# Causal decayed attention in front of a Strassen FFN: sequence chunks of 128 positions become chunks of 64 that lie two by two in the halves of the partitions

## The chip, the cores and the metric

The kernel runs on one core of one Trainium2 chip. The metric is the device time of one execution in microseconds (us). TensorE (PE) multiplies; it keeps a weight tile in its 128x128 array and streams columns past it, and its results go to PSUM, which has eight banks. VectorE (DVE) and ScalarE (ACT) take results out of PSUM, GpSimd (POOL) works on SBUF alone, and DMA queues are fed by SyncE (SP), ACT and POOL. Here a PE "record" is one line of the profile, a weight load with the matmul that uses it; each fp32 matmul of the program leaves two records, and a transpose through PE leaves one.

## The reference

```python
scores = scale * np.matmul(q, k.transpose(0, 1, 3, 2))       # q, k, v: 8 x 8 x 576 x 64 (batch, head, position, dim)
Dmat = np.where(rel >= 0, gamma[:, None, None] ** rel[None, :, :], 0.0)
attn = np.matmul(scores * Dmat[None], v)                     # gamma = 1 - 2 ** (-5 - head)
x = attn.transpose(0, 2, 1, 3).reshape(4608, 512)
out = (((x @ w1) * (x @ w2)) @ w3) @ w_out                   # 512 -> 1024 -> 1024 -> 512
```

All in float32. The decay is split by position into a factor on q and one on v, so inside a chunk only the causal mask is left, and everything before the chunk is summed in a 64x64 state (k transposed times v) for each head.

## The kernel before, in words

**Attention.** The 8 batches are 4 pairs. A pair's 576 positions are cut into a short chunk of 64 (c = 0) and four full ones of 128 (c = 1 to 4); `g` counts the 20 steps of (pair, chunk). A step has 16 units: 2 batches `b`, 4 pairs of heads `p`, 2 heads `j`. Head j of a pair lies in half j of the partitions (`heads[j]`). For a full chunk one step has four matmul stages of 16 matmuls, so 32 records each:

- `score` (L224): for every unit keys times queries, 64 rows deep, 128x128 out. The two heads use the two row halves of the array at once. The results (`sc`) are multiplied by the causal mask on DVE into `pm` (L236), four instructions of 128x512.
- `state` (L240): keys times values, 128 rows deep, 64x64 out, the two heads in the two column halves, summed in PSUM over a pair's chunks in `st` (one bank); ACT copies the sum to `sb` (L259) for the next chunk. The last chunk of a pair has none.
- `pv_state` (L264): state times queries, 64 deep, 64x128 out, four units at once in the four quarters of the array, into two banks `xps`.
- `pv` (L278): masked scores times values, 128 deep, 64x128 out, two column halves, added to `xps`; `evict` copies `xps` to `xT` on ACT (L306).

In the short chunk `score` and `pv` and `state` are 64x64 and use two quarters at once. Keys and queries are transposed for `score` either by PE (`front`, L207) or by DVE on blocks of 32 (`front_blocks`, L185).

**FFN.** Tokens go through Strassen products: `up` (L507) and, from the second half on, `up2` (L1008, weights streamed from HBM through the ring `ra`) for w1 and w2, `down` (L625) for the product w3*w_out, which is computed once (`w3_mm`). Each product is a run of records on the full array, 192 columns in `up` and `up2`, 256 in `down`; DVE, ACT and POOL add the products up.

**Order.** It is written out by hand, and each engine runs its instructions in the order of the program. The first pair's attention stands between weight conversions on DVE and ACT. From the second pair on, a step deals out some FFN items with `work(n)`, then runs `pv(g)` with its eviction, then `state(g + 1)` and `score(g + 1)` in one block, and goes on with the next items. The next chunk's loads, scalings and transposes stand between the items (`aside`, `beside`, `loads`). PSUM: `st` one bank, `acc` seven buffers; in the second half five, with two of `seed`.

Of the kernel before, what the change touches and what calls it, by code (L numbers as in the profile page):

```python
# [19 lines left out]
def kernel(  # L20
# [31 lines left out]
    G = NB2 * NC  # L52
    NB = 3
# [27 lines left out]
    acc = acc_part.enter_context(tc.tile_pool(name="acc", bufs=7, space=PSUM))  # L81
# [5 lines left out]
    def load(g, names, engine=nc.sync):  # L87
        i, c = divmod(g, NC)
        sz = sizes[c]
        src = {"k": k, "q": q, "v": v}  # L90
        for nm in names:
            t = pools["ld"].tile([P, 2 * H, D], F32, tag="ld_" + nm, name="ld_" + nm)
            engine.dma_start(
                t[:sz], src[nm][2 * i:2 * i + 2, :, starts[c]:starts[c] + sz, :].rearrange("b h p d -> p (b h) d"))
            live[nm, g] = t
# [11 lines left out]
                            base=0, pattern=[[1, P]], channel_multiplier=-1)  # L107

# [98 lines left out]
    def front(g, names="kq"):  # L207
        c = g % NC
        sz = sizes[c]
# [14 lines left out]
    def score(g):  # L224
        c = g % NC
        sz = sizes[c]
        kT, qT = live["kT", g], live["qT", g]
        pm = pools["fr"].tile([P, 2, 2, NP, P], F32, tag="pm", name="pm", bufs=1)
        for b in range(2):
            sc = [acc.tile([P, NP, P], F32, tag="acc", name="sc") for j in range(2)]  # L230
            for p in range(NP):
                for j, hs in enumerate(heads):
                    nc.tensor.matmul(sc[j][:sz, p, :sz], kT[hs, b, p, :sz], qT[hs, b, p, :sz],  # L233
                                     start=True, stop=True)
            for j in range(2):
                nc.vector.tensor_mul(pm[:sz, b, j, :, :sz], sc[j][:sz, :, :sz],  # L236
                                     mask[:sz, :sz].unsqueeze(1).to_broadcast([sz, NP, sz]))
        live["pm", g] = pm

    def state(g):  # L240
        c = g % NC
        sz = sizes[c]
        if c == NC - 1:
            return
        vs = live["v", g]
        kn = live["k", g]
        if c == 0:
            live["st"] = st_ps.tile([P, 2, NP, D], F32, tag="st", name="st")
        st = live["st"]

        for b in range(2):
            for p in range(NP):
                for j, hs in enumerate(heads):
                    h = b * H + 2 * p + j
                    nc.tensor.matmul(st[hs, b, p, :], kn[:sz, h, :], vs[:sz, h, :],  # L255
                                     start=(c == 0 and b == 0 and p == 0), stop=(c == NC - 2),
                                     skip_group_check=True)
        sb = pools["fr"].tile([P, 2, NP, D], F32, tag="sb", name="sb")
        nc.scalar.copy(sb, st)  # L259
        live["sb", g + 1] = sb  # L260

    bank_order = [(b, n) for b in range(2) for n in range(2)]

    def pv_state(g):  # L264

        sz = sizes[g % NC]
        qT = live["qT", g]

        banks = live["xps", g] = [acc.tile([P, 2, 2, P], F32, tag="acc", name="xps") for r in range(2)]
        if g % NC:  # L270
            for m, (b, n) in enumerate(bank_order):
                for r, j in ((0, 0), (0, 1), (1, 0), (1, 1)):
                    p = 2 * r + n
                    nc.tensor.matmul(banks[r][heads[j ^ r], b, n, :sz], live["sb", g][heads[j], b, p, :],  # L274
                                     qT[heads[j], b, p, :sz], start=(m == 0), stop=False,
                                     skip_group_check=True)

    def pv(g):  # L278

        if ("xps", g) not in live:  # L280
            pv_state(g)
# [3 lines left out]
        vs, pm, banks = live["v", g], live["pm", g], live["xps", g]  # L285
# [9 lines left out]
        for m, (b, n) in enumerate(bank_order):  # L295
            for r in range(2):
                for half in range(2):
                    p, j = 2 * r + n, half ^ r
                    nc.tensor.matmul(banks[r][heads[half], b, n, :sz], vs[:sz, b * H + 2 * p + j, :],  # L299
                                     pm[:sz, b, j, p, :sz], start=(c == 0 and m == 0), stop=True,  # L300
                                     skip_group_check=True)

        def evict():
            for x, to, fr, n in parts:
                for r in range(2):
                    nc.scalar.copy(  # L306
                        x[:, 2 * r:2 * r + 2, :, to:to + n].rearrange("p n b s -> p b n s"),
                        banks[r][:, :, :, fr:fr + n])

        return evict  # L310

# [192 lines left out]
    def up(i, n, fp, conv=0, tail=True, first=False):  # L507
# [28 lines left out]
        c = ffn.tile([P, 4, 2, TB], F32, tag="c", name="c", bufs=1)  # L536
        p1 = product(None, "A11", "B11")
        nc.scalar.copy(c[:, 0], p1)

# [7 lines left out]
        plus(p7 if first else product(None, "S3", "T3"), 2, 1)  # L547
        p5 = product(None, "S1", "T1")
# [4 lines left out]
        nc.scalar.copy(c[:, 0], p1)  # L553
        product(p5, "S4", "B22")
        plus(p5, 1, 1)

# [68 lines left out]
    def down(x, y, then=None, last=False):  # L625
# [35 lines left out]
        C11, C12, C21, C22 = (0, 0), (0, 1), (1, 0), (1, 1)  # L661
        product(1, "A11", "B11")
# [5 lines left out]
        if second:  # L668
            store()
            finish()  # L670
        product(7, "S3", "T3")
        if second:
            multiply()
# [8 lines left out]
        nc.scalar.copy(ot[:, 0, 0], ps[2])  # L682
        early = second or last or g >= 2 * NC - 1
# [9 lines left out]
        if second:  # L693
            store()
        product(3, "S4", "B22", on=5)
# [46 lines left out]
    pv_state(1)  # L742
# [47 lines left out]
    owed.append(2)  # L790
    pv(4)()
# [129 lines left out]
    def open_second():  # L921
# [3 lines left out]
        acc = ctx.enter_context(tc.tile_pool(name="acc", bufs=5, space=PSUM, reuse_waits="tile"))  # L925
# [82 lines left out]
    def up2(gr, n):  # L1008
# [34 lines left out]

        p1 = acc.tile([P, 2, TB], F32, tag="acc", name="up")
# [6 lines left out]
        nc.scalar.copy(c[:, 3], p5)  # L1051
        finish()
# [12 lines left out]
        plus(p1, 0, add)  # L1065
        product(p5, "S4", "B22")
# [12 lines left out]
        if aside:  # L1079
            aside.pop(0)()  # L1080

# [37 lines left out]
    g = NC  # L1119
# [4 lines left out]
    state(NC)  # L1124
    score(NC)
    scale_blocks(NC + 1)
    in_blocks = [u >= 2 * NC - 3 for u in range(G)] + [False] * 2
    first_pair = range(NC, 2 * NC - 1)
    for g in first_pair:
        n = (1, 1, 2, 2)[g - NC]  # L1130
        if not in_blocks[g + 2]:
            load(g + 2, "k")
            load_blocks(g + 2, "q")
        scale(g + 1, "v")
        if not in_blocks[g + 1]:
            front(g + 1, "k")
            front_blocks(g + 1, "q")
        half = (n + 1) // 2
        if in_blocks[g + 1]:
            scale_blocks(g + 1)  # L1140
            work(n - 1)
            aside.extend(lambda nm=nm: front_blocks(g + 1, nm) for nm in "kq")
            work(1)
            while aside:
                aside.pop(0)()
            half = 0
        if in_blocks[g + 2] and g + 2 < 2 * NC:
            load_blocks(g + 2, "q")
            load_blocks(g + 2, "k")
        work(half)  # L1150
        pv(g)()
        load(g + 2, "v", nc.scalar if in_blocks[g + 2] else nc.sync)
        if in_blocks[g + 2] and (g + 2) % NC != NC - 1:
            load(g + 2, "k")
        state(g + 1)
        score(g + 1)
        if not in_blocks[g + 2]:
            scale_blocks(g + 2)
# [7 lines left out]
        if not in_blocks[g + 1]:  # L1166
            work(n // 2)

    g = 2 * NC - 1
    work(1)  # L1170
    load_blocks(g + 1, "q")
    pv(g)()
    load(g + 2, "v", nc.scalar)
    load(g + 2, "k")
# [5 lines left out]
    g = 2 * NC  # L1180
    work(1)
    rest()
    aside.append(lambda: front_blocks(g, "q"))
    work(1)
    while aside:
        aside.pop(0)()
    front(g, "k")
    ready = {2 * NC + 3: 1, 3 * NC + 1: 2, G - 1: 3}

    whole = range(2 * NC + 1, 2 * NC + 4)  # L1190
    load_blocks(g + 1, "q")
    state(g)
    score(g)
    add_group(0)
    dealt = [3, 4, 4, 3, 3, 7, 7, 3, 7, 7]
    for g in range(2 * NC, G):
        n = dealt[g - 2 * NC]
        if g + 1 < G:
            beside.extend(lambda j=j: scale(g + 1, "v", range(j, j + H // 2)) for j in (0, H // 2))
# [3 lines left out]
            if g - 1 in ready:  # L1203
                token_forms(ready[g - 1])
            for nm in "qk":
                blocks_in = nm == "q" or g + 1 not in whole
                if blocks_in:
                    aside.append(lambda nm=nm: front_blocks(g + 1, nm))
                work(1)
                while aside:  # L1210
                    aside.pop(0)()
                if not blocks_in:
                    while loads:
                        loads.pop(0)()
                    front(g + 1, "k")
                if g + 2 < G and not (nm == "k" and g + 2 in whole):
                    load_blocks(g + 2, nm)
            work(tail)
            for left in (loads, beside):
                while left:  # L1220
                    left.pop(0)()
        else:
            work(n)
        pv(g)()
        if g in ready:
# [58 lines left out]
```

## Time and profile before

| what | us |
|---|---|
| median of 3 runs (851.12, 847.23, 860.4) | 851.12 |
| the profiled execution: its own time | 850.68 |
| its span, first to last instruction | 848.9 |
| records of `score`, `pv`, `pv_state`, `state`: PE busy | 40.2, 36.8, 17.7, 19.0 |
| PE busy in `down`, `up2`, `up` (their groups added up; groups overlap a little) | 230, 313, 165 |

The page gives each engine's busy time and its share of the span; the chain of waits follows what ended last, back from the end; a group line gives the shape of the weights (rows*columns), the output, the number of records, the time in which at least one of them ran, the mean duration of one, and the engine's idle time before them. Records overlap, so a group's busy time is less than number times mean. In the timeline the first column is the start in us from the span's start, the second the time to the end of the last record merged into that line. In the table of windows each engine has its busy time and, in brackets, how many of its instructions lie there.

### The profile page before, as it was taken

How to read it: one execution, taken by the hardware profiler on the slowest of the kernel's cores; microseconds unless marked ns; L12 is line 12 of the kernel's file. 1: busy time of each engine (PE TensorE's matmuls, PEld its weight loads, DVE VectorE, ACT ScalarE, POOL GpSimd, SP SyncE). 2: the span in 40 equal slices, each digit the busy share in tenths (PEclk: the TensorE clock that was granted, in tenths of full speed). 3: DMA queues.
4: the chain of work that ended last, by engine and by line, in shares of the span. 5: the costliest groups of instructions: out<-in, count | busy, mean ns of one | idle time of the engine just before them, and what ended most of it. 6: DMA issues, size and time to landing. Idle time of an engine off the chain costs nothing.

```text
span 848.9 us, 15774 instructions
## 1 busy us (share of the span) xinstructions
PE 819.3 (97%) x6085; PEld 738.1 (87%) x6085; DVE 541.2 (64%) x887; ACT 283.2 (33%) x581; POOL 325.6 (38%) x330
## 2 busy tenths in 40 slices
PE   7899999999999999979998999999999999999998
PEld 6889999644989998869998889998899998899987
DVE  4899999991644477615657644759735768446653
ACT  4777556670111101033343024342034331033300
POOL 1100010001104181395545935556916468445500
PEclk8999999999999999999999999999999999999999
DMA  9995454436046487979786147787275452245401
GB/s 193 217 224 128 77 150 125 126 98 112 1 98 125 75 220 251 307 209 220 190 229 167 44 93 228 201 238 177 58 156 183 140 208 69 77 148 189 159 25 51
DMA packets 201291, 126.96 MB, mean 150 GB/s; under 512 B 161272, under 2 KB 183032, under 8 KB 201216
## 3 DMA queue, kind: packets, MB, share of 16 engines
q1 hardware_dynamic: 170944, 50.14, 29.1%
q0 software_dynamic: 11776, 63.71, 23.0%
q10 hardware_dynamic: 18496, 12.10, 5.3%
q8 instruction: 48, 0.79, 0.4%
q14 instruction: 27, 0.22, 0.1%
HBM read 103.62 MB, written 22.28 MB: 148 GB/s over the span
## 4 chain that ended last, share of the span: by engine, by line
PE 79%; DMA 7%; DVE 7%; issue 3%; SPq 2%; ACT 1%; POOL 0%; ACTq 0%; DVEq 0%; POOLq 0%
PE po L637 24%; PE up L1028 15%; PE up L524 13%; PE seed L1028 11%; PE ps L477 6%; DMA ld_v<-in_v_dram 3%; PE xps L299 3%; PE sc L233 3%; DMA ra<-kept 2%; PE xps L274 1%; SPq L171 1%; DVE c L529 1%; DVE ab L1003 1%; DMA bl_q<-in_q_dram 1%; PE st L255 1%
## 5 line engine op out<-in xcount | busy, mean ns | idle before, releaser
L637 PE MATMUL po<-w3o,ab 128*128 128x256 f32 x552 | 125.0, 381 | 1.4 <-DVE ot L641 0.5
L637 PEld LDWEIGHTS po<-w3o,ab 128*128 128x128 f32 x552 | 103.9, 190 | 17.4 <-DVE ot L641 1.2
L1033 POOL TENSOR_TENSOR cc<-cc 128x384 f32<-128x384 f32 x112 | 109.3, 1001 | 4.1 <-ACT cc L1051 2.4
L1040 DVE TENSOR_TENSOR cc<-seed,cc 128x384 f32<-128x384 f32 x88 | 48.7, 553 | 72.9 <-PE seed L1028 68.5
L181 POOL TENSOR_TENSOR bl_q<-bl_q,gqs 128x512 f32<-128x512 f32 (+1 forms) x30 | 30.8, 1048 | 127.7 <-DMA bl_q<-in_q_dram 91.8
L939 POOL DMA_DIRECT2D ra<-kept x54 | 30.6, 567 | 124.1 <-PE seed L1028 103.3
L1028 PE MATMUL up<-xT,ra 128*128 128x192 f32 x384 | 74.2, 330 | 0.6 <-DMA ra<-kept 0.6
L1040 DVE TENSOR_TENSOR cc<-up,cc 128x384 f32<-128x384 f32 x88 | 48.4, 550 | 36.8 <-PE up L1028 31.5
L524 PE MATMUL up<-xT,wA 128*128 128x192 f32 x384 | 70.4, 327 | 0.0
L529 DVE TENSOR_TENSOR c<-up,c 128x384 f32<-128x384 f32 x80 | 44.0, 550 | 38.9 <-PE up L524 38.3
L1028 PEld LDWEIGHTS up<-xT,ra 128*128 128x128 f32 x384 | 64.4, 192 | 2.0 <-DMA ra<-kept 0.9
L236 DVE TENSOR_TENSOR pm<-sc,mask 128x512 f32<-128x512 f32 (+1 forms) x80 | 45.4, 626 | 32.1 <-PE sc L233 32.0
L637 PE MATMUL po<-wB,forms 128*128 128x256 f32 x288 | 65.2, 379 | 0.5 <-DVE forms L611 0.5
L524 PEld LDWEIGHTS up<-xT,wA 128*128 128x128 f32 x384 | 63.4, 190 | 1.1 <-issue 0.5
L637 PEld LDWEIGHTS po<-wB,forms 128*128 128x128 f32 x288 | 54.6, 190 | 8.2 <-PE po L637 0.8
L1047 ACT COPY seed<-up 128x384 f32<-128x384 f32 x56 | 25.9, 463 | 100.1 <-PE up L1028 46.6
L1028 PE MATMUL seed<-e,ra 128*128 128x192 f32 x256 | 52.9, 337 | 5.2 <-DVE cc L1040 2.9
L1028 PE MATMUL up<-ra 128*128 128x192 f32 x288 | 55.1, 328 | 1.9 <-DMA ra<-kept 1.9
L477 PE MATMUL ps<-wo,w3T 128*128 128x512 f32 x128 | 55.1, 592 | 0.0
L204 POOL TENSOR_TENSOR ld_v<-ld_v,gk 128x1024 f32<-128x1024 f32 (+1 forms) x9 | 17.1, 1899 | 90.5 <-DMA ld_v<-in_v_dram 90.5
L679 DVE TENSOR_TENSOR ab<-ab,forms 128x512 f32<-128x512 f32 x17 | 17.1, 1008 | 53.3 <-PE po L637 53.3
L1028 PEld LDWEIGHTS seed<-e,ra 128*128 128x128 f32 x256 | 43.7, 194 | 7.8 <-DVE cc L1040 3.6
(127 smaller groups left out, 1597.2 us busy)
## 6 DMA issues: line engine op xcount, KB each, us to landing
ra<-kept POOLq DMA_DIRECT2D x54, 896.0 KB, 5.0
raw<-in_moe_w_dram SPq DMA_DIRECT2D x72, 128.0 KB, 3.0
bl_q<-in_q_dram SPq DMA_DIRECT2D x216, 32.0 KB, 3.2
out_dram<-ot ACTq DMA_DIRECT2D x54, 128.0 KB, 2.3
bl_k<-in_k_dram SPq DMA_DIRECT2D x136, 32.0 KB, 2.4
raw<-in_moe_w_dram SPq DMA_DIRECT2D x16, 256.0 KB, 6.0
ld_k<-in_k_dram SPq DMA_DIRECT2D x8, 512.0 KB, 5.9
raw<-in_moe_w_out_dram SPq DMA_DIRECT2D x32, 128.0 KB, 2.7
```

The lines of the kernel that those rows point to most:

```text
L181: nc.gpsimd.tensor_tensor(out=part, in0=part, in1=gqs[:, :, n0:n0 + n].unsqueeze(3).to_broadcast([P, NP, n, BL]), op=ALU.mult)
L233: nc.tensor.matmul(sc[j][:sz, p, :sz], kT[hs, b, p, :sz], qT[hs, b, p, :sz], start=True, stop=True)
L236: nc.vector.tensor_mul(pm[:sz, b, j, :, :sz], sc[j][:sz, :, :sz], mask[:sz, :sz].unsqueeze(1).to_broadcast([sz, NP, sz]))
L477: nc.tensor.matmul(ps, live["w3T", ft][:, g, :], live["wo"][:, g, :], start=(g == 0), stop=(g == KF - 1))
L524: nc.tensor.matmul(ps[:, w, :], a[:, w, r, :], b[:, r, :], start=(new and w == r == 0), stop=(w == r == 1), skip_group_check=True)
L529: nc.vector.tensor_add(c[:, to], ps, c[:, sb])
L637: nc.tensor.matmul(ps[nm], a[A][:, f, :], live["W"][B][:, f, :], start=(f == 0 and not on), stop=(f == NP - 1), skip_group_check=True)
L939: engine.dma_start(ring[n % 3], kept[n % 14 // 7][nm])
L1028: nc.tensor.matmul(ps[:, w, :], weight_of(slot, a, w), B[b], start=(new and w == 0), stop=True, skip_group_check=True)
L1033: nc.gpsimd.tensor_tensor(out=o, in0=o, in1=i, op=ALU.add)
L1040: nc.vector.tensor_add(c[:, j], ps, with_add[:, j])
L1047: nc.scalar.copy(p6, p1)
```

## The change

A full chunk of 128 becomes two chunks of 64, `s` = 0 and 1, which lie in partitions 0 to 63 and 64 to 127. Every matmul of attention is now 64 rows by 64 columns of the array with 64 columns streamed, and successive ones go to the four quarters. Scores are computed only inside a chunk of 64, so half of the old score block and half of the `pv` depth fall away, and the state has to be known at each chunk of 64. The states of chunks in the lower and in the upper half are summed in two banks of `st`, and added on DVE. `pv` becomes two halves, `pv_half(g, False)` and `pv_half(g, True)`, which add to the same places from different row halves; between them a one-column ACT copy (`hand`) has to have read the first half's last result. `acc` loses one buffer.

```diff
+    CS = P // 2
-    acc = acc_part.enter_context(tc.tile_pool(name="acc", bufs=7, space=PSUM))
+    acc = acc_part.enter_context(tc.tile_pool(name="acc", bufs=6, space=PSUM))
...
+    nc.vector.tensor_copy(mask[CS:, :CS], mask[CS:, CS:])
...
     def score(g):
+        sc = [acc.tile([P, 2, NP, CS], F32, tag="acc", name="sc") for j in range(2)]
+        for b in range(2):
+            for p in range(NP):
+                for s in range(n):
+                    at_s = slice(s * CS, (s + 1) * CS)
+                    for j, hs in enumerate(heads):
+                        nc.tensor.matmul(sc[j][heads[s], b, p, :], kT[hs, b, p, at_s], qT[hs, b, p, at_s],
+                                         start=True, stop=True)
+        for j in range(2):
+            nc.vector.tensor_mul(
+                pm[:sz, j].rearrange("p b m x -> p (b m) x"), sc[j][:sz].rearrange("p b m x -> p (b m) x"),
+                mask[:sz, :CS].unsqueeze(1).to_broadcast([sz, 2 * NP, CS]))
...
     def state(g):
+        n = 1 if c == NC - 1 else chunks(g)
+            live["st"] = st_ps.tile([P, 2, 2, NP, D], F32, tag="st", name="st")
+                for s in range(n):
+                    for j, hs in enumerate(heads):
+                        nc.tensor.matmul(st[hs, s, b, p, :], kn[heads[s], h, :], vs[heads[s], h, :],
...
+        def ahead_of(g, s, odd):
+            sb = live["sb", g, s] = pools["fr"].tile([P, 2, NP, D], F32, tag="sb", name="sb")
+            if odd is None:
+                nc.scalar.copy(sb, st[:, 0])
+            else:
+                nc.vector.tensor_add(sb, st[:, 0], odd)
+        if n == 2 or c:
+            ahead_of(g, 1, live.get(("odd", g)))
+        if c < NC - 1:
+            odd = None
+            if n == 2:
+                odd = live["odd", g + 1] = pools["fr"].tile([P, 2, NP, D], F32, tag="odd", name="odd", bufs=1)
+                nc.scalar.copy(odd, st[:, 1])
+            live["next", g] = lambda: ahead_of(g + 1, 0, odd)
...
     def pv_state(g):
+            for s in range(2):
+                        nc.tensor.matmul(banks[r][heads[j ^ r], b, n, at_s], live["sb", g, s][heads[j], b, p, :],
+                                         qT[heads[j], b, p, at_s], start=(m == 0 and s == 0), stop=False,
+    def pv_half(g, second):
+        for m, (b, n) in enumerate(bank_order):
+            for r0, s in ((0, 0), (0, 1), (1, 0), (1, 1)):
+                j, r = s ^ second, r0 ^ second
+                half, p = j ^ r, 2 * r + n
+                if s < chunks(g):
+                    nc.tensor.matmul(
+                        banks[r][heads[half], b, n, s * CS:(s + 1) * CS], vs[heads[s], b * H + 2 * p + j, :],
+                        pm[heads[s], j, b, p, :], start=(c == 0 and m == 0), stop=True, skip_group_check=True)
+        if not second:
+            last = (heads[1 if c == 0 else 0], 1, 1, slice(sz - 1, sz))
+            nc.scalar.copy(hand[last[0]], banks[1][last])
...
+    def pieces(g, n, after=()):
+        def first():
+            score(g)
+            state(g)
+        def second():
+            pv_state(g)
+            pv_half(g, False)
+        def third():
+            pv_half(g, True)
+            if ("next", g) in live:
+                live["next", g]()
+            put_x(g)
+        plan.extend([] for _ in range(n))
+        plan[0].append(first)
+        plan[n - 1].append(second)
+        if g not in complete:
+            plan[n - 1].append(third)
+        plan[n - 1].extend(after)
+        if g in complete:
+            plan.append([third])
...
-        acc = ctx.enter_context(tc.tile_pool(name="acc", bufs=5, space=PSUM, reuse_waits="tile"))
+        acc = ctx.enter_context(tc.tile_pool(name="acc", bufs=4, space=PSUM, reuse_waits="tile"))
```

In the first pair `pv(g)` runs `pv_state` and the two halves one after the other; the state of a chunk now comes after its own scores in all pairs. From the second pair on a step's attention is three pieces (`first`, `second`, `third`): an item of `up`, `up2` or `down` takes them from a list at its start (`begin_item`) and runs one between two of its products at each `here()`. The first piece goes into a step's first item, the other two into its last; `put_x` is the old `evict`. A PE transpose of the next chunk's keys (`after`) follows the third piece. The values and keys of the next chunk are loaded at the top of a step, from the third pair on by POOL, and ACT's scaling of the values comes in four parts in place of two.

## The prediction

> **What bounds the kernel now.** I read the page's shares first, then the chain of waits, then attention's groups on PE by shape, then the timeline of one step.
>
> ```profile
> PE 819.3 (97%) x6085; PEld 738.1 (87%) x6085; DVE 541.2 (64%) x887; ACT 283.2 (33%) x581; POOL 325.6 (38%) x330
> ...
> PE 79%; DMA 7%; DVE 7%; issue 3%; SPq 2%; ACT 1%; POOL 0%; ACTq 0%; DVEq 0%; POOLq 0%
> ```
>
> PE is the bound: 97% busy and 79% of the chain. A microsecond of PE work saved is a microsecond of the end, unless a wait takes its place.
>
> ```profile
> L233 PE MATMUL sc<-qT,kT 64*128 64x128 f32 x512 | 35.5, 287 | 4.4 <-ACT qT L221 2.0 <-DVE kT L190 1.7 <-DVE cc L1040 0.7
> L299 PE MATMUL xps<-pm,ld_v 128*64 128x128 f32 x512 | 31.4, 276 | 0.0
> L274 PE MATMUL xps<-qT,sb 64*64 64x128 f32 x512 | 17.7, 275 | 0.0
> L255 PE MATMUL st<-ld_v,ld_k 128*64 128x64 f32 x384 | 13.6, 224 | 0.7 <-POOL ld_v L204 0.7
> ```
>
> These are the full chunks. Scores and `pv` fill two tiles of the array at a time and hold PE 35.5 and 31.4 us; `pv_state`, of the same 128 columns on four quarters, 17.7. One step in the timeline (PE's rows; start, length):
>
> ```profile
> 266.73 1.10 PE L274 MATMUL xps<-qT,sb 64*64 64x128 f32 x32
> ...
> 267.77 1.97 PE L299 MATMUL xps<-pm,ld_v 128*64 128x128 f32 x32
> ...
> 269.56 1.10 PE L255 MATMUL st<-ld_v,ld_k 128*64 128x64 f32 x32
> ...
> 270.60 2.06 PE L233 MATMUL sc<-qT,kT 64*128 64x128 f32 x32
> ...
> 272.58 1.57 PE L524 MATMUL up<-xT,wA 128*128 128x192 f32 x8
> ```
>
> From start to next start: 1.04 + 1.79 + 1.04 + 1.98 = 5.85 us. And the short chunk, two quarters at a time with 64 columns:
>
> ```profile
> 363.25 1.08 PE L255 MATMUL st<-ld_v,ld_k 64*64 64x64 f32 x29
> ...
> 364.23 1.10 PE L233 MATMUL sc<-qT,kT 64*64 64x64 f32 x31
> 365.25 0.59 PE L1016 MATMUL seed<-w3o,ident 128*128 128x384 f32 x1
> ```
>
> State and scores, 64 records in all, run into one another: both want tiles of 64x64, and no pause lies between them.
>
> **The price of a round.** I call the records that run abreast a round. `score` (16 rounds of 128 columns) takes 1.98, `pv_state` (8 rounds) 1.04: 0.94 / 8 = 0.118 us a round, and 0.10 is left as a tail to the next kind of tile. With 64 columns the joined block is 32 rounds in 2.00, so 0.059 a round with the same tail; `state` alone gives (1.04 - 0.10) / 16 = 0.059 too. Entering costs another 0.09 (8 `down` records started at 264.91, the first L274 at 266.73: 1.82, against 8 x 0.216, from 56 records in 12.09 in the chain).
>
> **Part by part.** First the main term, if four abreast with 64 columns cost what two abreast do, 0.059 a round.
>
> Full chunk, c = 1 to 3. Scores 64 records, state 64, `pv_state` 64, each half of `pv` 32; four abreast that is 16 + 16 + 16 + 8 + 8 rounds. Piece one: 32 x 0.059 + 0.10 = 2.0. Piece two: 24 x 0.059 + 0.10 = 1.52. Piece three: 0.57. Two more entries than now: 0.18. Sum 4.27 against 5.85: 1.58 saved, 12 times: 19.0.
> Last chunk, c = 4. Now 5.85 - 1.04 = 4.81. The change adds a state (one half, 32 records, two abreast, 16 rounds): again 4.27, 0.54 saved, 4 times: 2.2.
> Short chunk. Two abreast as now, but cut in three: 2.0 + 0.57 + 0.57 + 0.18 = 3.3 against 3 x 1.04 = 3.1: 0.2 lost, 4 times: 0.8.
> Sum: -20.4 us.
>
> Costs. (1) Between `pv`'s halves PE waits for ACT's `hand`: a matmul's drain (about 0.27, the mean of L274) and a tiny copy (between nothing and 0.59, ACT's 128x512 copy). From the second pair on FFN products stand in between (0.65 us in `up2`, 1.3 in `up`, 1.7 in `down`) and hide it; without that cover 15 x 0.6 = 9. In the first pair nothing stands between: 5 x 0.6 = 3. ACT's queue behind it is conversions, which have no slack to lose there. (2) `pv_state`'s second half needs the state just summed: `st` to copy or add (0.59) to PE. Later an item lies between; in the first pair key transposes (0.9 to 1.0) hide it except for c = 1: 1. (3) In the first pair DVE is busy 36.8 of 40.0 us from 45 to 85, and 23.2 of 25.0 after, with weights to convert. PE can't run far ahead of that, though DVE itself gets lighter (next point). (1) and (2) are 4 of that pair's 5.1 saved; I leave 1.
> (4) DVE: the mask takes two instructions of 0.62 a step in place of four, 1.24 saved in each of 16 steps; state adds take it back partly (six a pair, 0.6 each). What PE gets of it are its own waits for DVE around a step:
>
> ```profile
> PE seed L1028 <- DVE cc L1040: 2.9, 3, 1.3
> ...
> PE sc L233 <- DVE kT L190: 1.7, 1, 1.7
> ```
>
> Of these 4.6 us, smaller pieces with products between should take most: -3, between 0 and -5. (5) One buffer fewer in `acc`: no row shows PE waiting for a free one by that name; by position a product could wait one DVE add (0.55) per step: 0 to 8. I take 0, since five tiles of a `down` already share banks and adds run beside products. (6) Loads a step ahead, through POOL: the step is 20 us and more against 6 to land; 0, up to 2 in the second pair, whose steps are shortest (12 us).
> In all -20.4 + 4 - 3 = -19.4.
>
> **Where a rule of the skill speaks against it.** The row first: what the trace has of a quicker pace than 0.059 for two is the beginning of a block.
>
> ```profile
> 266.73:266.76 0.03, 0.03 (x4) 0.03 (x4) 1.00 1.40 546
> 266.73:266.83 0.10, 0.10 (x4) 0.10 (x8) 1.00 1.00 389
> ```
>
> Four loads and four matmuls begin within 0.03 us (first row of the table of windows: PE x4, PEld x4), four more loads within 0.10. So the quarters do take records at under 0.01 us apiece, for one round; the change needs 0.059 / 4 = 0.015 for 128 records on end. The Trainium skill's "TensorEngine Tiling (Array Packing)", section Instruction Overhead, gives each matmul about 60 cycles and warns against taking a tiling factor from a dimension that is already small; "TensorE: Matmul & The Clock Gate", section Back-to-back issue gap, puts the floor for 1 to 64 columns near 25 ns. If that floor holds across quarters, an estimate from that page is 3968 records of full chunks x 0.025 = 99 us plus tails, about 870 in all. No run here shows which.
>
> **Rivals.** *Issue sets the pace (slower).* Every sustained form in the trace lies at about 0.03 us a record: 0.118 / 4 on quarters, 0.059 / 2 on halves. That agrees with streaming columns, but also with a front end that can't deliver faster; then cutting records in half buys nothing and there are more of them. Full chunks have 256 records after (12 x) or 224 (4 x), 3968 in all. At 0.0295: step 256 x 0.0295 + 0.30 + 0.18 = 8.03, 12 x 2.18 = 26; last chunk 7.1, 4 x 2.3 = 9; short 0.8; with +4 and -3: 887. The sign turns where 12 x (256 x + 0.48 - 5.85) + 4 x (224 x + 0.48 - 4.81) + 0.8 + 1 = 0: 0.020 us a record. For it: no sustained row is faster. Against it: the window rows above. Lower end halfway between 0.020 and 0.0295: 868; I call it 877.
> *The gain is there and is eaten.* Uncovered `hand` 9, `acc` 8: -20.4 + 4 + 17 = about 851. For it: hand-made order with little slack; against: products stand between everywhere after the first pair.
> *Not what it says.* If the quarters ran two abreast only, rounds double: over 0.0295 a record, as the first rival.
>
> **The numbers.** The profiled execution took 850.7, close to the median 851.1 (847.2 to 860.4, a spread of 1.5%; 2% is about what can be told from no change). 850.7 - 19.4 = 831.3. This case's own range is 822 (waits gone: -5, no loss in the first pair) to 842. Chances: forecast 0.62 (0.50 of it under 834, which is 2% faster, 0.12 above), eaten or a pace near 0.020 0.10 (0.08 within 2%, 0.02 slower), issue-bound or not what it says 0.28. The range runs to 872, into the issue-bound case, and leaves out its upper part.
>
> **What would show it.** The score block of a full chunk with its state: 128 records in about 2.0 us (right), 3.8 (rival). A window of 0.06 us inside it should hold four matmuls. `pm` 2 x 0.62 a step. PE waits on `hand` in the first 85 us only. If the joined block takes more than 2.6 us, the forecast is wrong at its root.

## The result and the profile after

The changed kernel takes **886.49 us** (median of 4 runs, 880.9 to 887.8) against 851.36 for the kernel before, run beside it: a ratio of 1.042 [1.035, 1.048], 35 us slower where the prediction had 20 us faster. The profiled execution, 886.43 with a span of 884.7, is typical.

The page of after, first its shares, then the chain by engine:

```profile
PE 821.1 (93%) x8133; PEld 731.6 (83%) x8133; DVE 542.4 (61%) x872; ACT 288.3 (33%) x605; POOL 330.0 (37%) x336
...
PE 66%; DVE 8%; POOL 7%; DMA 7%; issue 6%; ACT 2%; SPq 2%; POOLq 0%; ACTq 0%; DVEq 0%
```

PE is busy as long as before (821.1 against 819.3), but idle for 884.7 - 821.1 = 63.6 us in place of 29.6. In the chain PE falls from 79% to 66%, and POOL, which had 0%, has 7%.

Attention's groups by shape, after (number of records | busy time, mean of one | idle time before them):

```profile
L306 PE MATMUL xps<-pm,ld_v 64*64 64x64 f32 x1152 | 30.8, 232 | 9.1 <-DVE cc L1118 4.2 <-ACT hand L313 2.1 <-issue 1.5
L260 PE MATMUL st<-ld_v,ld_k 64*64 64x64 f32 x1024 | 25.6, 232 | 7.5 <-DVE sb L269 4.2 <-POOL ld_v L210 3.3
L238 PE MATMUL sc<-qT,kT 64*64 64x64 f32 x1152 | 23.6, 221 | 3.9 <-ACT kT L226 1.7 <-DVE kT L196 1.1 <-ACT qT L226 0.6
L293 PE MATMUL xps<-qT,sb 64*64 64x64 f32 x1024 | 22.5, 230 | 13.4 <-DVE cc L1116 7.4 <-DVE sb L269 6.1
```

They are busy 102.5 us where the four stages had 113.7, and they stand idle ahead of it for 33.9, where the groups shown of before had 5.1. One step, after, in the timeline (PE's rows; start, length):

```profile
264.25 1.16 PE L238 MATMUL sc<-qT,kT 64*64 64x64 f32 x64
265.23 1.11 PE L260 MATMUL st<-ld_v,ld_k 64*64 64x64 f32 x64
266.27 1.99 PE L706 MATMUL po<-w3o,ab 128*128 128x256 f32 x8
268.20 1.16 PE L293 MATMUL xps<-qT,sb 64*64 64x64 f32 x64
269.18 0.65 PE L306 MATMUL xps<-pm,ld_v 64*64 64x64 f32 x32
269.76 1.99 PE L706 MATMUL po<-w3o,ab 128*128 128x256 f32 x8
271.68 0.80 PE L306 MATMUL xps<-pm,ld_v 64*64 64x64 f32 x32
272.41 1.78 PE L706 MATMUL po<-w3o,ab 128*128 128x256 f32 x7
```

Start to start: 2.02 for scores and state, 1.56, 0.73: 4.31 us, where the prediction had 2.0 + 1.52 + 0.57 = 4.09. A record of the first piece costs 2.02 / 128 = 15.8 ns. Each block of attention records also delays the records around it: wherever nothing else disturbs it, before and after alike, its first record starts 0.09 us late and the second FFN record behind it 0.10 us late. With one block a step before and three now, a step costs 5.85 + 0.20 = 6.05 us before and 4.31 + 0.60 = 4.91 here (4.80 in most steps, whose third piece takes 0.62). That is 1.1 to 1.2 us saved, where the prediction had 1.58. So the work did shrink, though by less than forecast, and something else ate it. PE's waits, after (total, times, longest):

```profile
PE xps L293 <- DVE cc L1116: 7.4, 5, 2.1
PE po L706 <- ACT ot L738: 7.3, 2, 6.8
PE xps L293 <- DVE sb L269: 6.1, 2, 3.5
PE xps L306 <- DVE cc L1118: 4.2, 1, 4.2
PE st L260 <- DVE sb L269: 4.2, 2, 2.2
```

None of these five stood in the profile before at such a size. Waiting is not all of it. The table of windows, after, around a `down` product that waited 1.96 us for DVE until 628.71 (busy times with numbers of instructions, then the granted clock, DMA share and GB/s):

```profile
626.00:629.40 3.40, 1.44 (x7) 0.99 (x6) 3.37 (x2) 0.37 (x1) 3.32 (x4) 1.00 0.28 63
629.50:632.90 3.40, 3.40 (x10) 2.69 (x9) 3.40 (x2) 0.00 (x0) 3.24 (x3) 0.50 0.01 2
632.90:636.30 3.40, 3.40 (x17) 2.88 (x16) 3.37 (x6) 0.00 (x0) 3.40 (x2) 1.00 0.00 0
```

The clock is 1.00 while PE waits (busy 1.44 of 3.40), then 0.50 for 3.40 us, in which ten records start, then 1.00 again, with 17 in the same length. Behind one wait of 1.96 us PE loses another 1.7 in busy time. Over the span the half clock holds 57 us after and 18 before (the trace's clock record added up), and PE is busy in 52.5 and 16.4 of them. At half speed half of that is lost: 26 us against 8. So the span is longer by 34 us of idle time (63.6 against 29.6) and 18 us of clock, and shorter by 16 us of work. That is why PE's busy total hides the saving: clock and work cancel in it.

### The profile page after: what moved, and what is told of

It reads as the page before. It is cut to its first block, busy times and chain, and to the rows that moved or that the text cites. A ratio compares the mean times of both kernels' runs of the same rounds, so it can differ in the third digit from the quotient of the medians.

```text
span 884.7 us, 19958 instructions
## 1 busy us (share of the span) xinstructions
PE 821.1 (93%) x8133; PEld 731.6 (83%) x8133; DVE 542.4 (61%) x872; ACT 288.3 (33%) x605; POOL 330.0 (37%) x336
## 3 DMA queue, kind: packets, MB, share of 16 engines
q8 instruction: 64, 1.05, 0.5%
## 4 chain that ended last, share of the span: by engine, by line
PE 66%; DVE 8%; POOL 7%; DMA 7%; issue 6%; ACT 2%; SPq 2%; POOLq 0%; ACTq 0%; DVEq 0%
PE po L706 23%; PE up L588 11%; PE up L1106 10%; PE seed L1106 9%; PE ps L541 6%; POOL cc L1111 5%; PE xps L306 2%; PE st L260 2%; PE sc L238 2%; DMA ld_v<-in_v_dram 2%; PE xps L293 2%; DMA out_dram<-ot 2%; DMA kept<-wA 1%; DVE c L593 1%; POOL bl_q L187 1%
## 5 line engine op out<-in xcount | busy, mean ns | idle before, releaser
L706 PE MATMUL po<-w3o,ab 128*128 128x256 f32 x552 | 137.9, 404 | 3.6 <-DVE ab L676 3.0
L706 PEld LDWEIGHTS po<-w3o,ab 128*128 128x128 f32 x552 | 109.0, 201 | 22.6 <-DVE ab L676 2.8
L588 PEld LDWEIGHTS up<-xT,wA 128*128 128x128 f32 x384 | 64.5, 193 | 0.8 <-issue 0.5
L706 PEld LDWEIGHTS po<-wB,forms 128*128 128x128 f32 x288 | 56.0, 195 | 10.3 <-issue 2.3
L1106 PEld LDWEIGHTS up<-ra 128*128 128x128 f32 x288 | 48.5, 192 | 2.1 <-issue 2.0
L710 DVE TENSOR_TENSOR ot<-po,ot 128x256 f32<-128x256 f32 x72 | 30.3, 421 | 32.5 <-PE po L706 31.7
```

Source lines behind the costliest of these rows:

```text
L588: nc.tensor.matmul(ps[:, w, :], a[:, w, r, :], b[:, r, :], start=(new and w == r == 0), stop=(w == r == 1), skip_group_check=True)
L706: nc.tensor.matmul(ps[nm], a[A][:, f, :], live["W"][B][:, f, :], start=(f == 0 and not on), stop=(f == NP - 1), skip_group_check=True)
L710: nc.vector.tensor_add(ot[:, to[0], to[1]], ps[nm], ot[:, sb[0], sb[1]])
L1106: nc.tensor.matmul(ps[:, w, :], weight_of(slot, a, w), B[b], start=(new and w == 0), stop=True, skip_group_check=True)
```

## The experiments

Eighteen kernels. Every ratio is to the kernel before on the same chip; in us it is multiplied by 851. "Step" is a step of attention, `sb` a summed state, `ot` the tile of `down`'s output.

**1. Fewer buffers, old kernel.** `acc` 7 and 5 to 6 and 4 in the kernel before, nothing else.

> The kernel before with one PSUM buffer of acc less (6 and then 4 in place of 7 and 5), nothing else. Theory A (the saved work is real, and waits ate it: the missing buffer, the state sums in VectorE's queue, and the halved clock behind every long wait): the kernel before must lose part of that too, by the changed kernel's waits of xps for cc (7.4 + 4.2 + 1.3 = 13 us, less since the order differs here) 5 to 15 us: 856 to 866. Theory B (the loss is the price of twice as many small records, in their supply and issue): the buffer costs nothing, 849 to 853.

1.006 [1.001, 1.011], about +5 us (1 to 9; the medians, 860.5 and 850.5, lie 10 apart). The buffer has a price, and in the old order it is small.

**2. No sum on DVE.** The sum of the two banks is left out (the odd chunks' state is then missing from the result); ACT copies one bank.

```diff
-                nc.vector.tensor_add(sb, st[:, 0], odd)
+                nc.scalar.copy(sb, st[:, 0])
```

> The changed kernel with the VectorE addition of the two state sums replaced by a ScalarE copy of the first sum alone; the states leave out the odd chunks' sum. The number of records stays. Theory A: PE's waits for sb (6.1 of pv_state and 4.2 of state) go or shrink to ScalarE's copy, and with them some 10 us at half clock, worth 5: 868 to 878. Theory B: 884 to 889.

877.21, 1.029 [1.023, 1.035], 11 us less than the change. The waits for `sb` on DVE are gone, but others take their place: PE is idle for 64.5 us, as long as in the change (63.6). What falls is the loss by the clock, from 26 us to 16 (PE is busy for 31.4 us at half clock).

**3. Second piece later.** An empty piece is put ahead of the second one, so that one more product runs first.

```diff
         plan[0].append(first)
+        if n != 2:
+            plan[n - 1].append(lambda: None)
         plan[n - 1].append(second)
```

> The changed kernel with an empty piece ahead of the second one (except in steps of two items): pv_state comes one place later in its item, behind two more products, and the second half at the item's end. Theory A: the previous item's additions are then done when pv_state asks for their buffer; its five waits for cc (7.4 us), the wait of the short chunk (4.2) and the wait for sb in step 9 (2.6) go, with the clock behind them: 866 to 876. Theory B: 884 to 889. A third possibility: the waits move on to the products that follow, 880 to 886.

880.93, 1.034 [1.026, 1.042]. `xps` in `pv_state` stands idle 4.5 us in place of 13.4, but `seed` waits for DVE's additions 9.0 in place of 3.5: the wait moved on.

**4. Sums taken early.** The next chunk's sum right behind the state, with three `sb` buffers, and the state of step 4 inside the item ahead of it.

```diff
...
-            live["next", g] = lambda: ahead_of(g + 1, 0, odd)
+            ahead_of(g + 1, 0, odd)
...
```

> The changed kernel with the state sum for the next chunk taken right behind the state (three buffers of sb in place of two) and not behind the third piece, and the state of step 4 moved up into the item ahead of it. Theory A: state's waits for sb (4.2 us, in the steps where the next chunk's state follows at once) and the 3.5 us of step 4 go, and the clock behind them (three windows of 3.4 us at half, worth up to 5): 874 to 881. Theory B: 884 to 889.

877.6, 1.029 [1.024, 1.035]. `st` no longer waits for `sb`. The sum in DVE's queue behind other work was worth 10 to 11 us, by this run and by the second (by the intervals 3 to 19). This run also has a third buffer and an earlier state in step 4, so it doesn't show the sum's place alone.

**5 to 7. GpSimd's queue.** In the changed kernel the values of step 9 arrive late, GpSimd's scaling of them stands in front of its writes of the kept weights (they begin at 330.2 us; before at 306.2), an output write issued in that stretch takes 8.6 us to land, where 2.3 is the median, and `po` waits 6.8 us for ACT's copy into `ot`. The fifth kernel moves that scaling behind the FFN items of steps 6 to 8, the sixth adds the edit of the fourth, the seventh that of the third too, with the first piece of step 5 one product later.

```diff
-            scale(g + 1, "v")
         pieces(g, n, k_pieces(g + 1))
...
         work(1)
+        if g > NC:
+            scale(g + 1, "v")
```

> The changed kernel with one move in steps 6 to 8: POOL's scaling of the next chunk's values stands behind the step's FFN items, not ahead of them right behind the load of those values. Theory A2 (the changed loads make POOL wait 10 to 12 us for a load that was just issued, and POOL's DMAs that write the weight forms to HBM wait behind it; the stores and loads of 335 to 385 us then collide): the writes begin where they began before the change, some 20 us earlier, PE's 6.8 us wait for ot goes, and of the 12.8 us that the changed kernel loses between FFN records 1200 and 1350 most comes back: 874 to 880. If those waits were of DMA bandwidth as such: 883 to 888.

> The move of POOL's scaling and the earlier sums of the states (with the state of step 4 earlier) together. Theory A: the two causes lie in different stages, so the gains add up: 9 of the sums alone and what POOL's move brings alone: 864 to 872. If waits only move on to the next late engine, less than the better of the two alone: 874 to 878.

> All of it: POOL's move, the earlier sums, the later second piece, and in step 5 the first piece behind a product, so that the key transposes' copies are covered. Theory A: 853 to 865; with every new wait gone it would be 831, and the buffer that acc lost still costs. If the waits move on: 868 or more.

896.11, 1.055 [1.046, 1.064]; 893.33, 1.049 [1.031, 1.067]; 879.91, 1.038 [1.030, 1.046]: no gain from the move. GpSimd's rows and one of PE's, fifth kernel:

```profile
319.71 3.20 POOL L960 DMA_DIRECT2D kept<-wA  x4
...
341.80 3.01 POOL L960 DMA_DIRECT2D kept<-wA  x4 [9.33 <-DVE wA L950]
```

```profile
347.52 1.97 PE L260 MATMUL st<-ld_v,ld_k 64*64 64x64 f32 x32 [7.29 <-POOL ld_v L210]
```

The writes begin 10.5 us earlier, as meant, and the wait for `ot` falls to 2.4. But one of the writes waits 9.33 us for DVE, and the scaling now stands behind it: PE gets the same wait from the other side. An in-order queue passes a late load on to whatever is behind it, in either order.

**8. Old order, new stages.** Stages, buffers and early sums of the fourth kernel in the order and with the loads of the kernel before; the next state stands between `pv`'s halves, so 256 records lie on end.

> The changed kernel's attention (chunks of 64, four quarters, two banks of sums, one buffer of acc less) in the order of the kernel before: pv of a step right after its FFN items, the next chunk's state between pv's two halves, then the next chunk's scores, in one block; loads, scalings and transposes where they were; sums of the states taken right behind the state, a step ahead of their use. Theory C (the quarters gain their 20 us; what the change lost, it lost by the new order: state, sums and pv of a step stand inside the step, with VectorE's and POOL's queues between them, and the loads that wait for pv come an item later): 835 to 846, the lost buffer's 5 to 10 us included. Theory D (the finer work loses them itself, through the buffer, the halves of pv and the sums on VectorE, wherever it stands): 860 or more.

878.73, 1.027 [1.018, 1.035]. The order alone is not to blame. PE's rows in one step:

```profile
432.21 1.16 PE L293 MATMUL xps<-qT,sb 64*64 64x64 f32 x64
433.19 0.65 PE L306 MATMUL xps<-pm,ld_v 64*64 64x64 f32 x32
433.66 1.11 PE L260 MATMUL st<-ld_v,ld_k 64*64 64x64 f32 x64
434.59 0.28 PE L306 MATMUL xps<-pm,ld_v 64*64 64x64 f32 x4
437.91 0.62 PE L306 MATMUL xps<-pm,ld_v 64*64 64x64 f32 x27 [3.03 <-issue]
```

In the middle of one run of `pv` records PE stops for 3.03 us, and the profile names no releaser ("issue"). In the trace a packet of the instruction queue runs from 435.00 to 436.43.

**9. Dense records.** Scores computed four times over from the second pair on, the rest as in the change.

> The changed kernel with every score block computed four times over from the second pair on (the same results into the same places), so that a full chunk has 256 score records and 64 state records on end instead of 64 and 64. Its span is longer by design; what counts is the length of the block. Theory I (TensorE's instructions arrive in 16 KB packets, 128 records each, and a run of dense records overtakes them): the 320 records take 7 us or more, with stalls of 1 to 3 us marked as issue inside the block, each ending 0.5 to 3 us after a packet of the instruction queue has begun, and the whole kernel takes 950 us or more. Rival (records at 0.0158 us can be delivered without end): 320 x 0.0158 = 5.1 us, no stall inside, 12 full chunks x 192 x 0.0158 + 3 short ones x 96 x 0.03 = +45 us, about 930.

One time, 955.9. The block of a step:

```profile
265.49 2.77 PE L238 MATMUL sc<-qT,kT 64*64 64x64 f32 x171
269.60 1.44 PE L238 MATMUL sc<-qT,kT 64*64 64x64 f32 x83 [1.33 <-issue]
...
270.89 0.85 PE L260 MATMUL st<-ld_v,ld_k 64*64 64x64 f32 x41
273.49 0.57 PE L260 MATMUL st<-ld_v,ld_k 64*64 64x64 f32 x21 [1.75 <-issue]
273.98 1.35 PE L706 MATMUL po<-w3o,ab 128*128 128x256 f32 x5
```

320 records take 273.98 - 265.49 = 8.49 us, not 5.1: the first 171 run at full pace, then PE stops twice with nothing to wait for. "issue" stalls of scores and states come to 37.6 us in all. The queue that carries instructions, from the page of the changed kernel:

```profile
q8 instruction: 64, 1.05, 0.5%
```

64 packets and 1.05 MB for 2 x 8133 loads and matmuls, so about 64 bytes an instruction and 16 KB, or 128 records, a packet. Before there were 48, and in this kernel, with 2592 records more, there are 84. PE's stops of over 0.4 us marked "issue" come to nothing before, 3.6 us after, 5.4 in the fourth kernel, 11.7 in the eighth and 38.4 in this one. Every one of them ends 1.2 to 1.9 us after such a packet does, and the two stops in the block above lie 128 records apart, one packet. So Theory I holds: where records come on end at 16 ns, PE is in the end as fast as its instructions arrive. How many pass first depends on where the packets lie: here the stop came after 171 records, in the eighth kernel's step above after 164, and one of the eighth's blocks, of 224 records, passed without one. The change spreads its records and mostly escapes this; the eighth kernel does not.

**10 and 11. Values of step 9 on ACT.** The fourth kernel with that one scaling on ACT; then with the edits of the third, and step 5's first piece one product later, as well.

```diff
...
-            scale(g + 1, "v")
+            if g != 2 * NC - 2:
+                scale(g + 1, "v")
         pieces(g, n, k_pieces(g + 1))
...
+        if g == 2 * NC - 2:
+            scale(g + 1, "v", True)
         drain(aside, att)
```

> The fourth experiment (chunk sums taken right behind the state, 877.6 us) with the scaling of the values of step 9 on ACT, behind the step's last item, instead of on GpSimd ahead of the writes of the kept weights. Theory P (one load a step later holds GpSimd's queue, the kept writes start late, the output write waits behind them and so does a down product, about 7 us and the half clock behind it): the writes begin before 322 us, the wait of po for ACT's copy to ot falls from about 7 us below 3, 866 to 872 us. Rival (the wait is taken over by DVE's or PE's next one, as when the scaling was only moved): 874 to 881 us with another wait of 3 us or more in the stretch 320 to 370.

> The run before it with the second piece one place later as well (an empty piece ahead of it in steps with more than two items... and in step 5 the first piece one place later). Theory P with waits that add up: 860 to 870 us, best of all variants. Rival (waits move on from one place to the next): 872 us or more.

887.15, 1.040 [1.032, 1.049], and 883.12, 1.035 [1.025, 1.046]. In the tenth kernel the `ot` wait falls to 2.3; `up` now waits 8.7 us for one of DVE's additions, and `st` 4.5 for ACT's scaling. The rival holds: the loads are late, and whoever scales them passes that on.

**12. The order alone.** The old stages (`score`, `state`, `pv_state` as the second piece, all of `pv` as the third, one bank of sums) and the old buffers in the order of the change.

```diff
...
-    acc = acc_part.enter_context(tc.tile_pool(name="acc", bufs=6, space=PSUM))
+    acc = acc_part.enter_context(tc.tile_pool(name="acc", bufs=7, space=PSUM))
...
-        acc = ctx.enter_context(tc.tile_pool(name="acc", bufs=4, space=PSUM, reuse_waits="tile"))
+        acc = ctx.enter_context(tc.tile_pool(name="acc", bufs=5, space=PSUM, reuse_waits="tile"))
```

> The order of the changed kernel alone: three pieces dealt between products, state behind scores, loads a step ahead, values scaled in four parts, but score, state and both pv stages as in the kernel before (128-position chunks, one state bank, seven and five acc buffers); the first piece is score and state, the second pv_state, the third all of pv. Theory O (the order is innocent, the loss comes with the new stages: sums on DVE, one buffer fewer, dense records): 845 to 856 us. Theory Q (the order itself brings the late loads and the queues that wait): 862 to 885 us, with the waits of po for ACT's ot copy and of L210-like scaling for its load as in the changed kernel.

870.67, 1.019 [1.011, 1.028]: +16.5 us, Theory Q. Where the loss stands is read from the sixteenth kernel, which has this order with one call moved and takes as long (870.12). Its writes of kept weights begin at 317.8, and matched with the kernel before by its FFN records it falls 9 us further behind between 306 and 345 us, of which 4 are won back by 394. Another 4 us or so are the price of smaller pieces: from 100 us on attention comes in 40 blocks in place of 19, and each of the 21 more costs 0.20.

**13. New stages, old order, dense blocks spread.** The eighth kernel with `pv`'s parts among the products of a step's last item.

> The new stages in the order and with the loads of the kernel before (as in the eighth experiment, sums taken right behind the state), but the 256 dense records of a step no longer on end: the two parts of pv go into the step's last item (96 records, a product or more, 32 records), and state and score follow behind that item (128). Theory R (two causes: the new order's later loads, which cost about 18 alone, and dense blocks that overtake the instruction fetch, about 30 in the eighth experiment): with both gone the 20 us of work come back less one buffer (5) and the first pair (8): 845 to 858 us, and less than 10 us of TensorE stalls with a fetch inside. Rival S (whatever is mended, DVE's and PSUM's waits move on): 866 to 880 us.

876.51, 1.028 [1.019, 1.036]. Stops marked "issue" fall from 11.7 to 2.0 us, but the time hardly moves, so neither theory's cause is the whole. Against the kernel before, 14 us are lost between its 286 and 324 us, where `up` waits 8.1 us for additions on DVE and the keys of step 9 come late (4.0 us; the change sums a state in a pair's last chunk, and has to load keys for it that the kernel before didn't).

**14 to 16. One transposition.** In step 5 DVE transposes step 6's queries at 262.1 us, before at 238.2, and the keys of step 7 wait for their buffer (loads begin at 263.4 us, before at 244.5). The call is put back ahead of the item: in the change, in the fourth kernel, in the order alone.

```diff
+        if g == NC:
+            front_blocks(g + 1, "q")
         pieces(g, n, k_pieces(g + 1))
         work(n - 1)
-        transposed(g + 1, "qk")
+        if g > NC:
+            transposed(g + 1, "qk")
```

> The changed kernel with one call moved: in the second pair's first step (step 5) the queries of step 6 are transposed by DVE ahead of the step's FFN item, as in the kernel before, not dealt into it. Theory V (the keys of step 7 share a ring of buffers with these queries; their 16 loads start at 263.4 us instead of 244.5, and SyncE's queue, 32 block loads of about 0.6 us a step, carries the delay through the pair to the values of step 9, to GpSimd and to the writes of the kept weights): the key loads start before 250 us, the values of step 9 before 312, the wait of po for ACT's ot copy goes from 7.3 below 3, and 870 to 877 us. Rival W (the pair is held by something else, the loads only follow): loads start earlier, 882 to 888 us.

> The run before with the chunk sums right behind the state as well (as in the fourth experiment, 877.6 us). Theory V: the two add up, 862 to 868 us. Rival W: 874 to 880 us.

> The order alone (the old stages in the new order, 870.7 us) with the queries of step 6 transposed ahead of the item. Theory V says that most of the 18 us of the order are this one call: 853 to 861 us. Rival W: 866 to 874 us.

887.68, 1.044 [1.039, 1.049]; 881.13, 1.036 [1.029, 1.043]; 870.12, 1.024 [1.018, 1.029]: nothing gained. In the first the keys start at 255.7 (not before 250, as Theory V wanted) and the next queries at 284.2, no earlier than in the change (281.2), since their buffer is freed inside a later item. Theory V fell.

**17. The order with fewer buffers.** The twelfth kernel with `acc` 6 and 4.

> The old stages in the new order (about 870 us) with the changed kernel's six and four acc buffers. It closes the square: before 851, fewer buffers in the old order 856, new order 870. Theory X (costs add up: order 18, buffer 5): 873 to 878 us, so that the new stages lie about 10 us above it instead of 20 below, and lose some 30 by themselves. Rival Y (the buffer is cheap in the old order and dear in the new one, whose pieces ask for PSUM beside the products): 888 us or more, so that the new stages as such still gain.

891.08, 1.045 [1.037, 1.053]: Rival Y. The buffer that costs some 5 us in the old order costs 18 to 22 in the new one (1.045 against 1.024 of the sixteenth kernel and 1.019 of the twelfth; with the intervals, 10 to 31). The loss lies in the second half, where `acc` has four buffers in place of five. Matched with the kernel before by the FFN records, this kernel is 10.7 us behind at 404 us and the sixteenth 11.6; from there to the end this one loses another 29.4, the sixteenth 8.3.

**18. The buffer given back to the change.** The states of odd chunks and their sum are left out, as in the second kernel, so the result is not complete.

```diff
...
-    acc = acc_part.enter_context(tc.tile_pool(name="acc", bufs=6, space=PSUM))
+    acc = acc_part.enter_context(tc.tile_pool(name="acc", bufs=7, space=PSUM))
...
-                for s in range(n):
+                for s in range(1):
...
-        acc = ctx.enter_context(tc.tile_pool(name="acc", bufs=4, space=PSUM, reuse_waits="tile"))
+        acc = ctx.enter_context(tc.tile_pool(name="acc", bufs=5, space=PSUM, reuse_waits="tile"))
```

> The changed kernel with one bank of state sums and seven and five acc buffers, as in the kernel before. It leaves out the states of the odd chunks and their sum (ACT copies the one bank, as in the second experiment, 877.2 us); the 32 state records left in a full chunk run two abreast in place of 64 four abreast, so TensorE's streaming time is the same. Theory Y (in the new order the lost buffer costs about 20 us, as the square of order and buffers says): 855 to 862 us, the waits of xps for the additions to cc gone. Rival X (the buffer costs about 5 and the rest is of the stages): 870 to 875 us.

**857.63**, 1.006 [1.002, 1.010], where the second kernel had 877.21. At 404 us this kernel is as late as the second (22.6 and 18.0 us behind the kernel before); from there to the end it wins back 12.5 us, and the second loses another 8.0. PE's waits from 400 us to the end, the four largest of the second kernel:

```profile
PE xps L293 <- DVE cc L1116: 7.4, 5, 2.1
PE po L706 <- DVE forms L680: 5.8, 1, 5.8
PE seed L1106 <- DVE cc L1118: 3.5, 4, 1.3
PE xps L306 <- DVE cc L1118: 2.6, 1, 2.6
```

and this one, all of 0.5 us and more:

```profile
PE seed L1106 <- DVE cc L1118: 4.9, 5, 1.4
PE up L1106 <- DMA ra<-kept: 4.7, 4, 2.3
PE sc L238 <- DVE kT L196: 1.1, 1, 1.1
PE po L706 <- DVE ab L676: 0.5, 1, 0.5
```

`xps` does not wait here any more. It isn't a pure test of the buffer: 384 state records are gone too (and 3 of the 64 packets), but the seventeenth kernel, where only the buffer differs, agrees. How the wait comes about is seen in the change at 436 us, first PE, then DVE:

```profile
434.45 0.81 PE L1106 MATMUL up<-e,ra 128*128 128x192 f32 x4
435.19 0.33 PE L293 MATMUL xps<-qT,sb 64*64 64x64 f32 x4
436.84 1.09 PE L293 MATMUL xps<-qT,sb 64*64 64x64 f32 x58 [1.31 <-DVE cc L1116]
```

```profile
435.19 0.56 DVE L1116 TENSOR_TENSOR cc<-up,cc 128x384 f32<-128x384 f32 x1
436.13 0.56 DVE L1116 TENSOR_TENSOR cc<-up,cc 128x384 f32<-128x384 f32 x1 [0.39 <-POOL cc L1111]
```

Four records go into the first bank of `xps`; by the wait, the second bank is still held by a product of `up2` that DVE adds up at 436.13. That addition itself waited for POOL's work on `cc`, which is how POOL comes into the chain. PE starts 0.15 us after the addition ends. Before, `xps` was taken between two items; now it is asked for in the middle of one, whose products hold the buffers.

## Why the prediction was wrong

*Main term (-20.4): the pace right, the size some 4 us too large.* A record takes 15.8 ns, and a step 4.31 us from start to start against 4.09. But a block of attention records costs 0.20 us beyond its own length, and the prediction counted the 0.09 ahead of it, not the 0.10 behind. In all the work shrank by 16 us. The rule that I weighed against it, the 25 ns floor for short streams in the Trainium skill's "TensorE: Matmul & The Clock Gate", Back-to-back issue gap, does not hold across quarters here, and the 870 that it gave is near the result by chance.

*(5) One buffer fewer, "I take 0", range 0 to 8: the step that failed most.* It costs 18 to 22 us in the new order, where `pv_state` asks for two banks in the middle of an item. I looked for the wait by name in the profile before, where there was none, and did not ask who asks for a buffer where in the new order. The 5 us of the first experiment show that the profile before could not have given the size; the order had to be gone through item by item.

*(6) Loads a step ahead, "0, up to 2": failed, with the order that I had costed at nothing.* The order with all else old costs 16.5 to 20 us. About 4 of them are its additional blocks. About 9 come where the late values of step 9 hold up GpSimd's writes, with 4 won back behind that; three ways to mend that only handed the wait on. I had counted the time from issue to landing, not what stands in each queue behind the late load. Why the loads are late is shown only for the first link (experiments 14 to 16); the rest of the order's price is not settled.

*(4) DVE's waits, -3: wrong sign.* I priced DVE's instructions by their length. The new sum stands behind other work in DVE's queue while PE waits for it (10.3 us in the profile after): 10 to 11 us by the second and fourth experiments.

*(1) to (3) The first pair, 4 us of cost: too little.* `hand` is right: 2.1 us in 5 waits, where I had 3. But by 104 us PE stands 6.2 us behind the kernel before, where I had it 1 ahead, so the costs there are 11 us; 3.5 us of it is one wait for `sb`.

*All of them: the clock.* I counted waits at their length. The half clock took 18 us more than before.

The sum now: -16 for the work with its blocks, +14 for the rest of the order, +20 for the buffer, +10 for the sum on DVE, +11 for the first pair, each with its share of the clock, make +39, and 35 was measured. The prices overlap (the first pair's is partly DVE's sum), so the agreement is rough. For the new stages in the old order (+23) it isn't closed: there the buffer and the sum are cheap, and what takes the gain back is only partly named (instruction fetch, loads in the second pair, the first pair).

*The rivals.* "Issue sets the pace" has the right side but the wrong mechanism: at 15.8 ns it fell, and its range held the time by other causes. Its grain of truth is the supply of instructions on long dense blocks. "The gain is eaten" had the right mechanism (`acc`) at 8 us, and gave 851.

No kernel that computes everything was faster than the one before.

## What to carry to other kernels

A saving on the busiest engine counts for what the buffers allow: before taking a PSUM buffer away, go through the new order item by item and ask who holds each buffer at the moment when the new piece wants one. Price an instruction put into an in-order queue by what stands ahead of it when its result is wanted, and a late load by everything behind its first reader, on whichever engine that is. Prices taken one at a time need not add up: order and buffer cost 38 us together, and 22 to 25 taken apart.

## What the runs showed of the hardware

- Four quarters take fp32 records of 64 x 64 x 64 at 15.8 ns each on end (128 in 2.02 us), but not without end: 320 took 8.49 us, with stops of 1.33 and 1.75 us, 128 records apart, while instructions come in packets of 16 KB (128 records).
- The profile marks such a stop "issue": all 20 of over 0.4 us in the ninth kernel end 1.2 to 1.6 us after an instruction packet ends.
- A change between the full array and its quarters costs 0.20 us there and back: 0.09 ahead of the block's first record and 0.10 at the second full-array record behind it, in every undisturbed block before and after.
- Short waits can bring the half clock: one of 1.96 us, in 3.40 us with PE busy for 1.44, was followed by 3.40 us at 0.50. The length of the wait doesn't decide it alone: behind one of 2.11 us that ended at 482.99, in 3.41 us with PE busy for 1.59, the clock stayed at 1.00. The Trainium skill's "TensorE: Matmul & The Clock Gate", HAM oscillation, warns of idle gaps over about 3.4 us; here a shorter one was enough.
